# Transform parts in the order sine, cosine, sine, cosine, and a row's write issued one ReLU later

## The chip, the cores and the metric

The kernel runs on one core of a Trainium2 chip. The metric is the device time of the kernel in microseconds (us). One further execution was recorded by the hardware profiler; all durations of single instructions come from it.

The engines are named as in the profile: PE is TensorE (matmuls; PEld are its weight loads), DVE is VectorE, ACT is ScalarE, POOL is GpSimd, SP is SyncE, which only issues DMAs here. A small q behind a name (ACTq) is that engine's sequencer, which works through the engine's instructions in their order; where one waits, all behind it wait.

## The reference

```python
def _attn_ref(x):                      # x: 8 x 3008 x 256
    X = np.fft.fft(x, axis=1)
    X = np.fft.fft(X, axis=2)
    return X.real.astype(np.float32)

def _moe_ref(x, w_in, w_out):          # x: 24064 x 256, w_in: 256 x 2048, w_out: 2048 x 256
    h = np.maximum(x @ w_in, 0.0)
    return (h * h @ w_out).astype(np.float32)
```

A two-dimensional Fourier transform of each of 8 batches, of which the real part is kept, then a feed-forward layer with a squared ReLU on all 24,064 rows.

## The kernel before

**Folding.** The input is real, so the output rows k and 3008 − k are found together. DVE folds each batch by symmetry (`fold_steps`), and the transform along the sequence is done for half of the rows: a cosine part `zc` and a sine part `zs`, both 128 partitions (features, folded too) by columns, one column for a pair of output rows. The transform along the features is merged into the weights of the first layer: `gh` has three blocks of 128 x 2048. For a pair, block 0 times `zc` plus block 1 times `zs` gives the first layer's result of row k (`pq`, L729 and L730). Block 2 times `zs`, added in the same PSUM tile, turns it into that of row 3008 − k (`turn`, L735). Block 2 is −2 times block 1, but for one feature, d=128, which lies in partition 0 of `zs` and keeps its sign.

**Units.** The columns are made in 16 units, two for each batch. In what follows the unit of the odd k is called early, that of the even k late. An early unit has 752 columns and 12 matmuls on `od`, a late one 753 columns and 20 matmuls on `xt`, `yt` and `spn` (both kinds L480). A unit is four parts: cosine or sine, each in a first half and a second half. `z_steps(u)(part, h)` gives the matmuls of one part: part 0 is the cosine, part 1 the sine, h the half. An early unit has three matmuls to each of the four. A late one has four to a cosine part and six to a sine part.

**A part's work.** The first half goes into a PSUM bank (pool `ps_z`, two buffers), and ACT copies it to `es` (L485). The second half is then added into the same bank, so its first matmul must wait for that copy. ACT copies the sum to `zc` or `zs` (L489): these are the unit's first 376 or 377 columns. DVE computes 2·es − sum (L496, `minus`): the other 376. Early units also need a column that a small matmul and a DVE copy make (`nyq`, L375 to L377, into the sine's half of `od`), late ones small POOL copies (`nyq8`, L423 to L425, into what the sine's first half reads).

**Windows and steps.** The columns are worked through in 25 windows, w = 0 to 24, most of them 512 wide (the first six are 240, 512, 376, 376, 512 and 448). A window has eight steps; step s does 256 of the 2048 hidden features for the window's columns. The code issues, engine by engine, in the order in which it is written: this is a schedule by hand (`manual_schedule`), so each engine runs its instructions in the order of the calls. In a usual step this is:

1. `pq(s)`: four matmuls into a PSUM tile (pool `ps_h`, two buffers).
2. `square(s, 0)`: the first ReLU on ACT (L739) into an `h1` tile (three buffers), then its square into `h2`, on DVE (L744) or, for the steps in `by_act`, on ACT (L742).
3. `others(s)`: fold work that is due; an eighth of the second layer of the window before (`ffn2_steps`: L618, 16 matmuls a group of 128 rows, in odd steps ACT's copy `osb`, L633, and the stores, L598, on SP's queue; `osb` has three buffers); and a seventh of the transform jobs of the unit that starts in the next window.
4. `turn(s)`: two matmuls; then `square(s, 1)`: the second ReLU and its square.

In windows 3 and 5 to 24, steps 1 up to 3, 4 or 5 are *halved* (`halved(w)`): ACT reads the PSUM tile only by copies, `sn` (L757, −2 times the sine's product) and `hd` (L766), and DVE forms the second row from the first (L774, L779, L787 to L789). There the d=128 feature must be added back: `row_sum` multiplies row 0 of `zs`, spread over all partitions in `eb`, by a weight (L774, twice a step) and adds it.

**The row.** `row_spread(w)` makes `eb` for window w in two DMAs: ACT's queue writes row 0 of `zs` to DRAM (`zr`, L579), and SP's queue, behind it, reads it back to all 128 partitions (`eb`, L581). It is called in step 6 of the window before. The write waits for the columns of `zs` that it reads, those of ACT and, where the window has some, those of DVE. In windows 0 and 4, two steps go together (`ng` = 2), and `row_spread` has another place.

**The order of the parts.** L721 lists a unit's jobs as cosine first half, sine first half, sine second half, cosine second half. `spread` deals the list in equal shares to steps 0 to 6 (in window 4 to steps 4 to 6, in window 1 all to step 6). Units are made in these windows:

| units | windows |
|---|---|
| early (12 matmuls) | 1, 6, 9, 11, 14, 17, 20 |
| late (20 matmuls) | 3, 4, 7, 10, 13, 16, 19, 22 |

The first early unit is made ahead of window 0, by calls of its own.

Of the kernel before, what the change touches and what calls it, by code (L numbers as in the profile page):

```python
# [19 lines left out]
def rev_dim(ap, i):  # L20

    dims = [list(d) for d in ap.ap]
    step, cnt = dims[i]
    dims[i] = [-step, cnt]
    return bass.AP(tensor=ap.tensor, offset=ap.offset + step * (cnt - 1), ap=dims)
# [3 lines left out]
def kernel(  # L29
# [51 lines left out]
    NW = len(wins)  # L81
# [372 lines left out]
    def zwin(w):  # L454
        if w not in zc:
            zc[w] = zp.tile([P, WN], F16, name="zc", tag="zc")
            zs[w] = zp.tile([P, WN], F16, name="zs", tag="zs")
        return zc[w], zs[w]
# [67 lines left out]
    def run(*jobs):  # L526
        for j in jobs:
            j()
# [45 lines left out]
    def row_spread(w):  # L574

        wn = wins[w][1]
        t = eb[w] = tmp.tile([P, WN], F16, name="eb", tag="kf")
        zr = drp.tile([1, WN], F16, name="zr", tag="zr")
        nc.scalar.dma_start(out=zr[0:1, 0:wn], in_=zwin(w)[1][0:1, 0:wn])  # L579
        src = zr[0:1, 0:wn]  # L580
        nc.sync.dma_start(out=t[:, 0:wn], in_=bass.AP(tensor=src.tensor, offset=src.offset, ap=[[0, P], [1, wn]]))  # L581
# [84 lines left out]
    def plan(w):  # L666

        if w < 3 or w == 4:
            return (), ()
        return PLAN[min(2, 2 * (w in fold_at) + (w in first_at) + (w in late_at))]  # L670

    def halved(w):

        return plan(w)[0]
# [4 lines left out]
    for w in range(NW):  # L679
# [4 lines left out]
        lo, hi = 0, NST - 1  # L684
# [4 lines left out]
        elif w == 1:  # L689
# [3 lines left out]
            lo, hi = 6, 7  # L693
# [24 lines left out]
        zj, zl = [], []  # L718
        for u in need[w + 1]:
            zu = z_steps(u)  # L720
            zj += [(zu, 0, 0), (zu, 1, 0), (zu, 1, 1), (zu, 0, 1)]  # L721
        f2 = ffn2_steps(*old) if old else []
        phs = {}

        def pq(s):
            ph = phs[s] = ps_h.tile([P, 2, 512], F32, name="ph", tag="psh")
            for a in range(2):
                f0 = (2 * s + a) * P
                nc.tensor.matmul(ph[:, a, 0:wn], gh[:, 0, f0 : f0 + P], zcw[:, 0:wn], start=True, stop=False)  # L729
                nc.tensor.matmul(ph[:, a, 0:wn], gh[:, 1, f0 : f0 + P], zsw[:, 0:wn], start=False, stop=True)  # L730

        def turn(s):
            for a in range(2):
                f0 = (2 * s + a) * P
                nc.tensor.matmul(phs[s][:, a, 0:wn], gh[:, 2, f0 : f0 + P], zsw[:, 0:wn], start=False, stop=True, skip_group_check=True)  # L735

        def square(s, sg):
            h1 = h1p.tile([P, 2, 512], F16, name="h1", tag="h1")
            nc.scalar.activation(h1[:, :, 0:wn], phs[s][:, :, 0:wn], AF.Relu)  # L739
            hv = rev_dim(h1[:, :, 0:wn], 2) if sg else h1[:, :, 0:wn]  # L740
            if sg == 0 and s in by_act:
                nc.scalar.activation(h2[:, 2 * s : 2 * s + 2, 0:wn], hv, AF.Square)  # L742
                return []
            return [lambda: nc.vector.tensor_tensor(h2[:, 2 * s : 2 * s + 2, sg * wn : (sg + 1) * wn], hv, hv, op=ALU.mult)]  # L744
# [5 lines left out]
        def half_q(s):  # L750
            ph = phs[s] = ps_h.tile([P, 2, 512], F32, name="ph", tag="psh")
            for a in range(2):
                f0 = (2 * s + a) * P
                nc.tensor.matmul(ph[:, a, 0:wn], gh[:, 1, f0 : f0 + P], zsw[:, 0:wn], start=True, stop=True)  # L754
            i = ROT[0] % 2
            sn = sns[s] = const.tile([P, 2, 2, WN], F16, name=f"sn{i}", tag=f"w16_{i}")
            nc.scalar.activation(sn[:, 0, :, 0:wn], ph[:, :, 0:wn], AF.Copy, bias=0.0, scale=-2.0)  # L757

        def half_p(s):
            ph, sn = phs[s], sns[s]  # L760
            for a in range(2):
                f0 = (2 * s + a) * P
                nc.tensor.matmul(ph[:, a, 0:wn], gh[:, 0, f0 : f0 + P], zcw[:, 0:wn], start=False, stop=True, skip_group_check=True)  # L763
            hd = tmp.tile([P, 2, 2 * WN], F16, name="hd", tag=("tt", "tm")[ROT[0] % 2])
            ROT[0] += 1
            nc.scalar.activation(hd[:, :, 0:wn], ph[:, :, 0:wn], AF.Copy, bias=0.0, scale=1.0)  # L766
            hds[s] = hd

        def row_sum(s):

            sn = sns[s]

            def row(a):
                nc.vector.tensor_scalar(out=sn[:, 1, a, 0:wn], in0=eb[w][:, 0:wn], scalar1=wv[:, 2 * s + a : 2 * s + a + 1], scalar2=None, op0=ALU.mult)  # L774

            return [
                lambda: row(0),
                lambda: row(1),
                lambda: nc.vector.tensor_tensor(sn[:, 0, :, 0:wn], sn[:, 0, :, 0:wn], sn[:, 1, :, 0:wn], op=ALU.add),  # L779
            ]  # L780

        def halves(s):

            sn, hd = sns[s], hds[s]
            hv = hd[:, :, 0 : 2 * wn]
            return [
                lambda: nc.vector.tensor_tensor(rev_dim(hd[:, :, wn : 2 * wn], 2), hd[:, :, 0:wn], sn[:, 0, :, 0:wn], op=ALU.add),  # L787
                lambda: nc.vector.tensor_scalar(out=hv, in0=hv, scalar1=0.0, scalar2=None, op0=ALU.max),  # L788
                lambda: nc.vector.tensor_tensor(h2[:, 2 * s : 2 * s + 2, 0 : 2 * wn], hv, hv, op=ALU.mult),  # L789
            ]  # L790

        def others(s):
            for j in at[s]:
                j()
            for j in spread(f2, s, NST):
                j()
            for j in post[s]:
                j()
            if s == lo:
                zl[:] = [j for zu, part, h in zj for j in zu(part, h)]  # L800
            if s >= lo:
                for j in spread(zl, s - lo, hi - lo) if s < hi else []:
                    j()


        ng = 2 if w == 0 or wins[w - 1][1] < 384 < wn else 1
        for s0 in range(0, NST, ng):
            ss = range(s0, s0 + ng)
            left = halves(s0 - 1) if s0 - 1 in two else []
            if s0 in two:  # L810
                half_q(s0)
                for j in [j for p in zip(left or [run] * 3, row_sum(s0)) for j in p]:
                    j()
                others(s0)
                half_p(s0)
                continue
            for s in ss:
                pq(s)
            for s in ss:
                run(*(left[0:2] + square(s, 0) + left[2:3]))  # L820
            if s0 == hi - 1 and ng == 1 and w + 1 < NW and halved(w + 1):
                row_spread(w + 1)
            others(s0)
            for s in ss:
                turn(s)
            for s in ss:
                run(*square(s, 1))
            for s in ss[1:]:
                others(s)
            if s0 < hi <= s0 + ng - 1 and w + 1 < NW and halved(w + 1):  # L830
                row_spread(w + 1)
# [33 lines left out]
```

## Time and profile before

| | us |
|---|---|
| time, median of 3 runs | 620.66 (619.44 to 620.81) |
| the profiled execution | 619.07 |
| its span, first to last instruction | 617.1 |
| PE busy | 587.7 |
| ACT busy | 517.6 |
| DVE busy | 498.6 |
| POOL busy | 77.3 |
| DMA engines, mean rate | 81 GB/s |

The span is what the profile divides into busy and idle time; 1.97 us of the execution lie outside it. TensorE's granted clock was 0.998 of full speed. The times of matmuls overlap, as each is listed from its start to the end of its results, so a stall is read from the starts of two matmuls in a row. In the list of waits a line says who waited for whom, with the total in us, the number of waits and the longest. In a timeline a line gives the start, the duration, the engine, the line of the kernel and the tiles (what is written, then what is read), and in brackets the engine's idle time before it and what ended it; "x2" are two such instructions in a row.

A window of 512 columns takes about 24.4 us: the late units' transforms in windows 10, 13, 16 and 19 start at 242.27, 315.68, 389.08 and 462.49 us, three windows apart.

### The profile page before, as it was taken

The page shows a single profiled execution, that of the slowest core. Times are in us where ns is not written, and L with a number is a line of the kernel's source. Part 1 is how long each engine was busy: PE and PEld are TensorE (multiplying, and loading weights), DVE is VectorE, ACT ScalarE, POOL GpSimd, SP SyncE. Part 2 cuts the span into 40 slices and gives each one's busy share as a digit, 9 for nine tenths or more (in the row PEclk, how much of TensorE's full clock was granted, in tenths as well). Part 3 has the DMA queues.
Part 4 walks back from the last instruction along what each step waited for, and adds up shares of the span by engine and source line. Part 5 has one row for each costly group of instructions (what it writes and reads, how often), then busy time and mean ns, then how long its engine had stood idle before and what let it go on. Part 6 is the DMA issues. An engine that isn't in the chain of part 4 may idle for free.

```text
span 617.1 us, 11655 instructions
## 1 busy us (share of the span) xinstructions
PE 587.7 (95%) x4400; PEld 424.0 (69%) x4400; DVE 498.6 (81%) x870; ACT 517.6 (84%) x673; POOL 77.3 (13%) x125
## 2 busy tenths in 40 slices
PE   5899999999899999999999999999999999999996
PEld 2456776776677777677776767677776776766785
DVE  7886688696888887969978799768987698797980
ACT  7786788888889889889898898888987988979871
POOL 5352200002001022020011100211000200100000
PEclk9999999999999999999999999999999999999999
DMA  8937121164214522631145311552212411111122
GB/s 145 219 71 144 61 68 35 43 150 104 52 38 83 151 85 57 134 112 59 37 106 121 91 49 46 98 131 81 52 31 66 111 52 44 55 47 42 58 58 65
DMA packets 39593, 50.22 MB, mean 81 GB/s; under 512 B 4572, under 2 KB 33393, under 8 KB 39537
## 3 DMA queue, kind: packets, MB, share of 16 engines
q0 software_dynamic: 9344, 22.14, 17.9%
q1 hardware_dynamic: 29923, 27.11, 15.3%
q8 instruction: 34, 0.56, 0.4%
q10 hardware_dynamic: 270, 0.23, 0.1%
q14 instruction: 22, 0.18, 0.1%
HBM read 36.29 MB, written 27.86 MB: 104 GB/s over the span
## 4 chain that ended last, share of the span: by engine, by line
PE 57%; ACT 15%; DVE 13%; issue 8%; DMA 5%; POOL 1%; SPq 0%; ACTq 0%; DVEq 0%; POOLq 0%
PE po L618 33%; ACT h L739 7%; PE ph L735 4%; PE ph L763 4%; PE ph L729 4%; PE ph L730 4%; PE ph L754 4%; PE pz L480 2%; DVE hd L787 2%; DMA out_dram<-osb 2%; DVE h L744 2%; ACT osb L633 2%; ACT hd L766 2%; DVE hd L788 2%; DVE sn L779 2%
## 5 line engine op out<-in xcount | busy, mean ns | idle before, releaser
L618 PE MATMUL po<-wout,h 128*128 128x256 f16 (+1 forms) x3024 | 361.7, 273 | 0.0
L618 PEld LDWEIGHTS <-h 128*128 128x128 f16 (+1 forms) x3024 | 296.5, 98 | 71.3
L739 ACT ACTIVATE h<-ph 128x1024 f16<-128x1024 f32 (+4 forms) x236 | 217.0, 961 | 27.4 <-PE ph L735 18.3
L744 DVE TENSOR_TENSOR h<-h 128x1024 f16<-128x1024 f16 (+4 forms) x173 | 109.5, 641 | 67.4 <-ACT h L739 65.3
L766 ACT ACTIVATE hd<-ph 128x1024 f16<-128x1024 f32 (+3 forms) x82 | 81.4, 992 | 28.1 <-PE ph L763 27.3
L789 DVE TENSOR_TENSOR h<-hd 128x2048 f16<-128x2048 f16 (+3 forms) x82 | 96.5, 1177 | 0.4
L729 PE MATMUL ph<-zc,gh 128*128 128x512 f16 (+4 forms) x236 | 85.2, 363 | 1.3 <-ACT h L739 0.5
L730 PE MATMUL ph<-zs,gh 128*128 128x512 f16 (+4 forms) x236 | 85.1, 363 | 0.4 <-ACT zs L489 0.4
L757 ACT ACTIVATE sn<-ph 128x1024 f16<-128x1024 f32 (+3 forms) x82 | 81.2, 991 | 0.4 <-DVE hd L787 0.2
L787 DVE TENSOR_TENSOR hd<-hd,sn 128x1024 f16<-128x1024 f16 (+3 forms) x82 | 54.9, 670 | 20.0 <-ACT hd L766 14.3
L735 PE MATMUL ph<-zs,gh 128*128 128x512 f16 (+4 forms) x236 | 65.4, 363 | 4.8 <-ACT h L739 3.2
L633 ACT ACTIVATE osb<-po 128x512 f32<-128x512 f32 (+3 forms) x95 | 54.6, 579 | 18.2 <-PE po L618 13.2
L742 ACT ACTIVATE h<-h 128x1024 f16<-128x1024 f16 (+3 forms) x63 | 64.8, 1029 | 2.0
L774 DVE TENSOR_SCALAR sn<-eb,wv 128x512 f16<-128x512 f16 (+3 forms) x164 | 54.3, 342 | 4.2 <-DMA eb<-zr 2.8
L779 DVE TENSOR_TENSOR sn<-sn 128x1024 f16<-128x1024 f16 (+3 forms) x82 | 54.5, 664 | 2.2
L788 DVE TENSOR_SCALAR hd<-hd 128x2048 f16<-128x2048 f16 (+3 forms) x82 | 54.7, 667 | 0.7
L763 PE MATMUL ph<-zc,gh 128*128 128x512 f16 (+3 forms) x164 | 47.3, 370 | 1.7 <-ACT sn L757 1.0
L754 PE MATMUL ph<-zs,gh 128*128 128x512 f16 (+3 forms) x164 | 47.4, 370 | 0.0
L730 PEld LDWEIGHTS <-gh 128*128 128x128 f16 x236 | 23.0, 97 | 25.5 <-issue 2.4
L729 PEld LDWEIGHTS <-gh 128*128 128x128 f16 x236 | 23.0, 97 | 24.8 <-DVE zc L496 1.1
L423 POOL COPY xt<-xt 128x2 f16<-128x2 f16 x16 | 6.0, 402 | 212.2 <-DVE xt L406 212.2
L735 PEld LDWEIGHTS <-gh 128*128 128x128 f16 x236 | 22.3, 97 | 13.2 <-issue 7.9
(121 smaller groups left out, 374.2 us busy)
## 6 DMA issues: line engine op xcount, KB each, us to landing
out_dram<-osb SPq DMA_DIRECT2D x77, 128.0 KB
xo<-in_x_dram POOLq DMA_DIRECT2D x7, 768.0 KB
scr<-ev POOLq DMA_DIRECT2D x8, 390.0 KB, 3.3
eb<-zr SPq DMA_DIRECT2D x18, 128.0 KB
rb<-scr POOLq DMA_DIRECT2D x16, 130.0 KB
out_dram<-osb SPq DMA_DIRECT2D x12, 94.0 KB
w<-in_moe_w_in_dram POOLq DMA_DIRECT2D x2, 512.0 KB
wout<-in_moe_w_out_dram POOLq DMA_DIRECT2D x1, 1024.0 KB
```

The costliest lines, as they stand in the source:

```text
L618: nc.tensor.matmul(po[0:m, j * D : (j + 1) * D], h2[:, fc, q : q + m], wout16[:, fc, :], start=(fc == 0), stop=(fc == NFC - 1))
L729: nc.tensor.matmul(ph[:, a, 0:wn], gh[:, 0, f0 : f0 + P], zcw[:, 0:wn], start=True, stop=False)
L730: nc.tensor.matmul(ph[:, a, 0:wn], gh[:, 1, f0 : f0 + P], zsw[:, 0:wn], start=False, stop=True)
L735: nc.tensor.matmul(phs[s][:, a, 0:wn], gh[:, 2, f0 : f0 + P], zsw[:, 0:wn], start=False, stop=True, skip_group_check=True)
L739: nc.scalar.activation(h1[:, :, 0:wn], phs[s][:, :, 0:wn], AF.Relu)
L744: return [lambda: nc.vector.tensor_tensor(h2[:, 2 * s : 2 * s + 2, sg * wn : (sg + 1) * wn], hv, hv, op=ALU.mult)]
L754: nc.tensor.matmul(ph[:, a, 0:wn], gh[:, 1, f0 : f0 + P], zsw[:, 0:wn], start=True, stop=True)
L757: nc.scalar.activation(sn[:, 0, :, 0:wn], ph[:, :, 0:wn], AF.Copy, bias=0.0, scale=-2.0)
L763: nc.tensor.matmul(ph[:, a, 0:wn], gh[:, 0, f0 : f0 + P], zcw[:, 0:wn], start=False, stop=True, skip_group_check=True)
L766: nc.scalar.activation(hd[:, :, 0:wn], ph[:, :, 0:wn], AF.Copy, bias=0.0, scale=1.0)
L787: lambda: nc.vector.tensor_tensor(rev_dim(hd[:, :, wn : 2 * wn], 2), hd[:, :, 0:wn], sn[:, 0, :, 0:wn], op=ALU.add),
L789: lambda: nc.vector.tensor_tensor(h2[:, 2 * s : 2 * s + 2, 0 : 2 * wn], hv, hv, op=ALU.mult),
```

## The change

Two edits. In the job list of a unit, the first two entries change places, so that the parts come as sine first half, cosine first half, sine second half, cosine second half. And in step 6 of a window, `row_spread` is called behind `turn` and the second `square`, instead of ahead of `others`.

```diff
@@ -718,7 +718,7 @@
         for u in need[w + 1]:
             zu = z_steps(u)
-            zj += [(zu, 0, 0), (zu, 1, 0), (zu, 1, 1), (zu, 0, 1)]
+            zj += [(zu, 1, 0), (zu, 0, 0), (zu, 1, 1), (zu, 0, 1)]
         f2 = ffn2_steps(*old) if old else []
@@ -818,13 +818,13 @@
                 run(*(left[0:2] + square(s, 0) + left[2:3]))
-            if s0 == hi - 1 and ng == 1 and w + 1 < NW and halved(w + 1):
-                row_spread(w + 1)
             others(s0)
             for s in ss:
                 turn(s)
             for s in ss:
                 run(*square(s, 1))
+            if s0 == hi - 1 and ng == 1 and w + 1 < NW and halved(w + 1):
+                row_spread(w + 1)
             for s in ss[1:]:
                 others(s)
```

Every engine has as many instructions as before. PE runs the same matmuls with the first halves exchanged, and in late units, whose sine parts are longer, other matmuls fall into a step. On ACT the copies `es` change places in the same way, and the write of the row stands one ReLU later in 20 of 21 windows (window 4 has its own place for it). On SP the broadcast moves behind four stores in window 6 and keeps its place elsewhere.

## The prediction

> **What bounds the kernel now.** I read the shares of busy time first, then the list of waits, then the timelines of TensorE (PE), ScalarE (ACT) and VectorE (DVE) in each window that runs a transform.
>
> ```profile
> PE 587.7 (95%) x4400; PEld 424.0 (69%) x4400; DVE 498.6 (81%) x870; ACT 517.6 (84%) x673; POOL 77.3 (13%) x125
> ...
> PE pz L480 <- ACT es L485: 7.6, 9, 1.0
> ACT osb L633 <- DMA zr<-zs: 1.8, 1, 1.8
> DVE sn L774 <- DMA eb<-zr: 2.8, 2, 2.2
> ```
>
> PE has almost no idle time, so only what delays PE counts, and the first wait is nearly pure PE time: nine times a transform's matmul waits for ACT to copy the bank that it adds to (7.6 us). Six of the nine are alike, in step 3 of windows 7, 10, 13, 16, 19 and 22 (178.46 to 545.18 us). PE in window 10:
>
> ```profile
> 250.71 0.25 PE L480 MATMUL pz<-cos,spn 128*128 128x94 f16 x2
> 251.93 0.24 PE L480 MATMUL pz<-sin,xt 128*128 128x188 f16 x1 [0.98 <-ACT es L485]
> ...
> 258.26 0.25 PE L480 MATMUL pz<-cos,spn 128*128 128x94 f16 x2
> 258.35 0.24 PE L480 MATMUL pz<-cos,xt 128*128 128x188 f16 x1
> ```
>
> Where nothing waits, the matmul behind such a pair starts 0.09 us after it (258.26 to 258.35); in step 3 it starts 1.22 us after (250.71 to 251.93). So one stall costs PE 1.13 us. ACT meanwhile runs an output copy and then the copy that is awaited:
>
> ```profile
> 250.91 0.60 ACT L633 ACTIVATE osb<-po 128x512 f32<-128x512 f32 x1 [0.24 <-PE po L618]
> 251.40 0.48 ACT L485 ACTIVATE es<-pz 128x377 f32<-128x377 f32 x1
> 252.64 1.02 ACT L766 ACTIVATE hd<-ph 128x1024 f16<-128x1024 f32 x1 [0.76 <-PE ph L763]
> ```
>
> ACT idles 0.76 us behind it, for PE: neither is the bound there, they wait for each other in turn. The second wait stands once on ACT, in step 6 of window 6:
>
> ```profile
> 162.50 0.21 ACTq L579 DMA_DIRECT2D zr<-zs  x1
> 162.90 0.60 ACT L633 ACTIVATE osb<-po 128x512 f32<-128x512 f32 x1 [1.78 <-DMA zr<-zs]
> ...
> 165.75 0.59 PE L735 MATMUL ph<-zs,gh 128*128 128x512 f16 x2 [1.73 <-ACT h L739]
> ...
> 162.22 0.60 DVE L496 SCALAR_TENSOR_TENSOR zs<-es,pz 128x102 f16<-128x102 f32 x2
> 162.74 0.69 DVE L744 TENSOR_TENSOR h<-h 128x1024 f16<-128x1024 f16 x1
> ```
>
> The row's write needs the sine columns that DVE finishes at 162.4; ACT's queue stands still behind it, both ReLUs come late, and PE waits 1.73 us at the next turn.
>
> **Part 1, the order of the four transform parts.** No instruction is added or removed: per unit the same matmuls, two es copies and two L496s. Before, the sine's second half came straight behind its first, and had to wait for ACT's copy of the same bank. After, four (late units) or three (early units) cosine matmuls stand between, and the sine's copy has all of a step or more to run. A late unit's 20 matmuls are dealt over steps 0 to 6 as 2, 3, 3, 3, 3, 3, 3: the sine's first six end in step 2 instead of step 3, so the wait in step 3 goes; the cosine's copy takes the sine's old place in ACT's queue, and its second half comes two steps later. The sums, by window:
>
> - Windows 7, 10, 13: the 1.13 us goes, and with it 0.12 us in step 2 (PE L763 waits for ACT's sn copy at 248.10: the es copy leaves ACT's step 1 for step 2, which has no output copy). 1.25 us each, 3.75 us. What is late next is DVE, which runs without a gap from 247.2 to 260.4 and does not get faster. ReLU tiles have three buffers: the first ReLU of step 6 (260.7) needs the one that DVE's L744 reads until 259.1, so there is 1.55 us of cover. DVE itself gets 0.36 us (hd of step 1 starts 0.36 us earlier, no copy of 0.48 us ahead of it), so 1.25 us fits.
> - Window 16: the same 1.25 us, but window 17 gives some back. There DVE waited for the row's broadcast already (first L774 at 418.82, 1.34 us idle), on transfers that crowd the queue and do not shift with PE. I take DVE 0.9 us later against PE; its L789 of step 5 ends 437.97 and PE's output matmuls need it at about 438.4, so 0.4 us is covered, 0.5 is paid: 0.7 us kept.
> - Window 19: DVE starts 2.19 us late (below), and its L744 ends at 480.70, just as the ReLU of step 6 starts (480.88). No cover: 0.1 us.
>
> ```profile
> 467.23 0.62 DVE L774 TENSOR_SCALAR sn<-eb,wv 128x512 f16<-128x512 f16 x2 [2.19 <-DMA eb<-zr]
> ...
> 557.97 0.60 DVE L496 SCALAR_TENSOR_TENSOR zc<-es,pz 128x16 f16<-128x16 f32 x2
> ...
> 558.19 0.39 PE L729 MATMUL ph<-zc,gh 128*128 128x512 f16 x1
> ```
>
> - Window 22 has five halved steps, and the next window needs 16 of the columns that DVE makes last: the last two lines above, L496 at 557.97 and the matmul behind it at 558.19 (due at 558.12). Only DVE's own 0.36 us is gained.
> - Window 3: stall of 0.74 us, but its end waits for DVE too (0.34 us at 95.66, DVE without a gap from 81.4): 0.
> - Window 4: 0.74 us at 112.95; DVE idles 1.67 us at 115.27, so it is kept: 0.74.
> - Window 1: all twelve matmuls in one step. Two es copies in a row end at 50.40 and 50.88; the sine's second half may then start at 50.47 instead of 50.93: 0.45.
>
> The sine going first asks for its inputs a step earlier. The Nyquist column (L377) ends 1.4 to 2.5 us before the first transform matmul of early units, GpSimd's copies (L424) 1.1 to 5 us before that of late units. I take 0, and up to 1 us a unit if that cover goes.
>
> **Part 2, the row's write.** 20 of 21 writes move behind one ReLU (window 4 has its own place for it). The issue itself is 0.215 us on ACT's sequencer, beside a running instruction: 0.
>
> In window 6 the hold moves from in front of output copy, cosine copy and second ReLU to in front of the next ReLU. These three then run 161.1 to 163.0 while the wait ends at 162.5. But the next ReLU needs a buffer that DVE's L744 frees at 163.43, so it starts 163.5 instead of 164.66: 1.15 us of the 1.73.
>
> The price is a later row: 0.2 to 1.4 us (to the start of the next L739 in each window). It lands 1.1 us after its issue in quiet stretches (window 8: issued 211.17) and up to 3.65 in busy ones (window 16: 408.54, SP's broadcast behind it at 412.24). The broadcast lands mostly 3.0 to 3.5 us after that (5.4 for window 19, where SP's issue waits behind a store until 461.67, so that a later write costs nothing there). Before DVE's first L774 this leaves 1.5 to 5.3 us in all windows but 5, 17 and 19. So it is hidden but for window 17 (counted above); unhidden, it would be up to 1.4 us of DVE time a window, of which chains of five halved steps cover 0.4 (window 17) to 0.9 (window 14). On SP the broadcast passes four stores in window 6 only, with 3.9 us to spare: 0. In window 2 output buffers wait for stores behind the broadcast (ACT idle 0.90 us at 75.51): −0.2.
>
> [...]
>
> **Sum:** 3.75 + 0.7 + 0.1 + 0.36 + 0 + 0.74 + 0.45 + 1.15 − 0.2 = 7.05 us. The profiled execution took 619.07 us (span 617.1 and 1.97 around it): 612.0. It lies 1.6 us under the median of 620.66, from which the forecast for the median is **613.6 us**.
>
> **Rivals.**
> - *DVE is the bound in all late units* (chance 0.20). For: its chains without a gap, 3.9 us a halved step against PE's 2.9. Against: no L618 waits for DVE, idle time in steps 6 to 0. Each of six windows then gains 0.36, windows 2 and 17 lose 0.7: 2.2 + 0.74 + 0.45 + 1.15 − 0.7 = 3.8, 616.8 us.
> - *All covers hold* (0.12). 6 × 1.25 + 2 × 0.74 + 0.45, and both holds of ACT that reach PE (1.73, and 0.45 before 557.69): 11.6 us, 609.1. For: DVE has idle time in every window. Against: the buffers and columns named above.
> - *The reorder only moves the wait* (0.05): the second half of the cosine waits instead, or the sine waits for its inputs (up to 1 us in each of nine units). Against: two steps of cover. Within 0.2% of before, about 620.
> - *Slower: the late row starves DVE* (0.08). Place: the first L774 of a window. If each broadcast took window 19's 5.4 us instead of 3.2 and the write came 1.4 later, the twelve windows with under 3.6 us to spare would start DVE some 1.75 us late, less 0.6 of cover: 14 us lost against 7 gained, 627.6. It decides from about 0.7 us of uncovered lateness in each of twelve. Against: PE did not stall behind the 2.19 us at 467.
>
> **How the numbers follow.** The forecast (611 to 616) has 0.55. The next two, 609.1 with 0.12 and 616.8 with 0.20, lie in the range, with 0.6 us below and the spread of the three runs (1.4 us) above: 608.5 to 618.2, which leaves out the last two rivals and some edges. 0.2% (1.2 us) is about what a measurement of this kernel can tell from no change. Faster 0.87, same 0.05, slower 0.08.
>
> **What would show it.** Right: PE's waits for es under 1 us in all, no gap in step 3 of windows 7 to 16, ACT's 1.78 us gone and some 0.7 us left before the turn in step 7 of window 6. Wrong: PE L618 or ACT L739 waiting for DVE in windows 8 to 18, or L774 waiting for the broadcast in more than four windows.

## The result and the profile after

The changed kernel took 610.2 us (median of 4 runs, 609.66 to 612.05); the kernel before took 620.05 us beside it (4 runs, 619.21 to 620.81). The ratio is 0.9847, 95% interval 0.982 to 0.9874: faster, by 9.85 us between the medians (1.5%). The profiled execution took 609.66 us (before 619.07), its span is 607.6 us (617.1).

The shares of busy time of the changed kernel, and its list of waits (total us, times, longest us):

```profile
PE 585.7 (96%) x4400; PEld 423.4 (70%) x4400; DVE 497.9 (82%) x870; ACT 518.0 (85%) x673; POOL 79.0 (13%) x125
```

```profile
DVE sn L774 <- DMA eb<-zr: 5.8, 3, 3.0
...
PE ph L763 <- ACT sn L757: 2.1, 6, 0.6
...
ACT sn L757 <- DVE hd L787: 1.9, 3, 0.9
```

PE has the same matmuls. Its idle time, the span less its busy time, fell from 29.4 to 21.9 us; its busy time is 2.0 us less, as a part of each stall is listed as busy (of the 1.13 us between the starts, 0.98 were listed as idle). `PE pz L480 <- ACT es L485`, 7.6 us before, is gone from the list, and so is ACT's wait of 1.8 us for `zr`. The last two lines have grown, from 1.0 and 0.2 us, and DVE's wait for the broadcast from 2.8 to 5.8 us.

**Where the time went, window by window.** A window's length is the distance from its first `pq` matmul on PE to the next window's. It repeats to 0.01 us from one execution to the next almost everywhere, so it tells far smaller differences than the time of the whole kernel. In all windows that are not listed it changed by less than 0.01 us.

| window | change of length, us | forecast of the step |
|---|---|---|
| 1 | −0.47 | −0.45 |
| 2 | 0.00 | +0.2 |
| 3 | −0.03 | 0 |
| 4 | −0.96 | −0.74 |
| 6 | −1.85 | −1.15 |
| 7 | −1.14 | −1.25 |
| 10, 13, 16 | −1.25 each | −1.25 each |
| 17 | **+1.57** | +0.5 |
| 18 | −0.04 | 0 |
| 19 | **−1.25** | −0.1 |
| 22 | −0.30 | −0.36 |
| 23 | −0.51 | 0 |

They sum to 8.7 us. The other 0.8 us of the 9.5 us between the two spans lie behind PE's last matmul: there the span of before goes on for 5.32 us and that of the changed kernel for 4.56, because before's last output copy waited for a store (1.59 us). Of the eleven runs below, ten end in 4.57 to 4.73 us and one, with the changed order, in 5.52, so I take this for chance and no part of the change.

**Step 3 of a late unit.** PE in window 10 of the changed kernel, at the place where it stood still for 0.98 us before:

```profile
252.59 0.25 PE L480 MATMUL pz<-cos,spn 128*128 128x94 f16 x2
252.68 0.24 PE L480 MATMUL pz<-cos,xt 128*128 128x188 f16 x1
252.76 0.59 PE L735 MATMUL ph<-zs,gh 128*128 128x512 f16 x2
```

The starts are 0.09 and 0.08 us apart and there is no bracket: the cosine's matmuls run through.

**Step 6 of window 6.** First ACT, then DVE, then PE:

```profile
160.43 1.02 ACT L739 ACTIVATE h<-ph 128x1024 f16<-128x1024 f32 x1
161.08 0.21 ACTq L579 DMA_DIRECT2D zr<-zs  x1
161.39 1.02 ACT L739 ACTIVATE h<-ph 128x1024 f16<-128x1024 f32 x1
```

```profile
160.79 0.60 DVE L496 SCALAR_TENSOR_TENSOR zs<-es,pz 128x102 f16<-128x102 f32 x2
161.31 0.68 DVE L744 TENSOR_TENSOR h<-h 128x1024 f16<-128x1024 f16 x1
```

```profile
162.47 0.59 PE L735 MATMUL ph<-zs,gh 128*128 128x512 f16 x2
```

The second ReLU (160.43) now runs ahead of the row's write. The first of the two L496 makes the sine columns that the row needs and ends at 161.04, the write goes at 161.08, and the next ReLU follows at 161.39 with nothing waited for. It starts while DVE is still busy with L744 (161.31 to 161.99), and PE's next turn at 162.47 has no idle time ahead of it.

**Window 17.** DVE, ACT and PE of the changed kernel, where the new waits are:

```profile
412.27 0.61 DVE L774 TENSOR_SCALAR sn<-eb,wv 128x512 f16<-128x512 f16 x2 [2.98 <-DMA eb<-zr]
...
417.45 0.69 DVE L787 TENSOR_TENSOR hd<-hd,sn 128x1024 f16<-128x1024 f16 x1
```

```profile
418.24 1.02 ACT L757 ACTIVATE sn<-ph 128x1024 f16<-128x1024 f32 x1 [0.76 <-DVE hd L787]
...
421.90 1.02 ACT L757 ACTIVATE sn<-ph 128x1024 f16<-128x1024 f32 x1 [0.94 <-DVE hd L787]
```

```profile
419.31 0.59 PE L763 MATMUL ph<-zc,gh 128*128 128x512 f16 x2 [0.57 <-ACT sn L757]
...
422.97 0.59 PE L763 MATMUL ph<-zc,gh 128*128 128x512 f16 x2 [0.57 <-ACT sn L757]
```

This is a chain to be read from top to bottom: the broadcast lands late, so DVE starts 2.98 us after it could. There are two `sn` tiles (L755), so ACT may write a step's `sn` only when DVE's L787 has read that of two steps before, and it waits 0.76 and 0.94 us. PE needs ACT to have read its PSUM tile, and stands still twice, 0.73 us each time by the distance of its starts; 0.11 us more go in the step ahead of these.

### The profile page after: what moved, and what is told of

It is laid out like the page before. It is cut to its first block, busy times and chain, and to the rows that moved or that the text cites. A ratio compares the mean times of both kernels' runs of the same rounds, so it can differ in the third digit from the quotient of the medians.

```text
span 607.6 us, 11662 instructions
## 1 busy us (share of the span) xinstructions
PE 585.7 (96%) x4400; PEld 423.4 (70%) x4400; DVE 497.9 (82%) x870; ACT 518.0 (85%) x673; POOL 79.0 (13%) x125
## 4 chain that ended last, share of the span: by engine, by line
PE 57%; DVE 16%; ACT 10%; issue 9%; DMA 6%; POOL 1%; SPq 0%; ACTq 0%; DVEq 0%; POOLq 0%
PE po L618 33%; PE ph L735 5%; PE ph L729 5%; PE ph L730 5%; ACT h L739 5%; PE ph L763 3%; DVE hd L787 3%; DVE sn L779 3%; PE ph L754 3%; DVE hd L788 3%; DVE sn L774 2%; DMA eb<-zr 2%; PE pz L480 2%; ACT sn L757 2%; DMA out_dram<-osb 2%
## 5 line engine op out<-in xcount | busy, mean ns | idle before, releaser
L618 PE MATMUL po<-wout,h 128*128 128x256 f16 (+1 forms) x3024 | 361.7, 273 | 0.0
L618 PEld LDWEIGHTS <-h 128*128 128x128 f16 (+1 forms) x3024 | 296.6, 98 | 71.3
L739 ACT ACTIVATE h<-ph 128x1024 f16<-128x1024 f32 (+4 forms) x236 | 217.3, 961 | 26.3 <-PE ph L735 15.4
L744 DVE TENSOR_TENSOR h<-h 128x1024 f16<-128x1024 f16 (+4 forms) x173 | 109.1, 642 | 61.6 <-ACT h L739 54.8
L789 DVE TENSOR_TENSOR h<-hd 128x2048 f16<-128x2048 f16 (+3 forms) x82 | 96.6, 1178 | 0.4
L787 DVE TENSOR_TENSOR hd<-hd,sn 128x1024 f16<-128x1024 f16 (+3 forms) x82 | 55.0, 671 | 18.4 <-ACT hd L766 10.7
L774 DVE TENSOR_SCALAR sn<-eb,wv 128x512 f16<-128x512 f16 (+3 forms) x164 | 54.6, 343 | 5.8 <-DMA eb<-zr 5.8
```

Of the source, the lines that this page charges most:

```text
L618: nc.tensor.matmul(po[0:m, j * D : (j + 1) * D], h2[:, fc, q : q + m], wout16[:, fc, :], start=(fc == 0), stop=(fc == NFC - 1))
```

## The experiments

The theory for part 1, called D in the expectations: the stall goes because other matmuls stand between the halves of one part. The rival: because the sine comes first. For window 17 there are three: the later write itself starves DVE (L), the read-back stands in a queue behind stores (Q), the two `sn` tiles pass the lateness on (S). All changes of window lengths below are against the kernel before.

### One part at a time

The order alone (the row's write at its old place), and the row's write alone (the old order of parts):

```diff
             if s0 == hi - 1 and ng == 1 and w + 1 < NW and halved(w + 1):
                 row_spread(w + 1)
             others(s0)
```

> Only the parts' order is changed; the row's write stays ahead of the transform jobs of step 6. Theory L (the late write is what starves VectorE in window 17): window 17 gives back at most 0.5 us instead of 1.57, windows 1, 4, 7, 10, 13, 16 and 19 keep their gains (0.47, 0.96, 1.14, 1.25 each), window 6 keeps its hold (0 instead of 1.85 gained); sum about 620.05 - 8.3 = 611.8, or near the changed kernel. Rival Q (the broadcast lands late in window 17 because the queues do not move with TensorE): window 17 gives back about 1.5 us here too, sum about 613.

> Only the row's write is moved. Both theories: window 6 gains 1.85 us, the stalls at the es copies stay (9 waits, 7 to 8 us). Theory L: VectorE's wait for the broadcast in window 17 grows from 1.3 us towards 3 and TensorE pays up to 1.5 us there; total 618.2 to 620. Rival Q: window 17 as before, total about 618.0. In neither is it slower than before.

The order alone: 611.2 us, ratio 0.987 (0.9845 to 0.9894). The row alone: 616.29 us, ratio 0.995 (0.9933 to 0.9967). With the order alone, ACT's wait in window 6 stays:

```profile
ACT osb L633 <- DMA zr<-zs: 1.8, 1, 1.8
```

The windows show what belongs to which part. Window 6 (−1.86) and window 23 (−0.52) belong to the row: with the order alone both are 0.00. Everything else is the order's, but for window 17: +0.59 with the order alone, 0.00 with the row alone, +1.57 with both. So the two parts add up in all windows but this one. There the order alone lies between what L (at most 0.5) and Q (about 1.5) had me expect, and the row alone, where DVE waits 1.29 us (before 1.34), speaks against L.

### Is it the sine first, or something between the halves?

```diff
-            zj += [(zu, 1, 0), (zu, 0, 0), (zu, 1, 1), (zu, 0, 1)]
+            zj += [(zu, 1, 0), (zu, 0, 0), (zu, 0, 1), (zu, 1, 1)]   # e3: sine outside, cosine halves adjacent
+            zj += [(zu, 0, 0), (zu, 1, 0), (zu, 0, 1), (zu, 1, 1)]   # e5: alternating, cosine first
```

> Order sine first half, cosine first half, cosine second half, sine second half, row's write as in the changed kernel. Theory D (what counts is that other matmuls stand between a part's two halves): the cosine's second half now stands right behind its first, so the stalls are back, for the cosine: 1.13 us each in windows 7, 10, 13, 16, 19, 0.74 in window 4, 0.3 to 0.5 in window 1; about 616 to 617. Rival (sine first, or the row's place, is what gains): no stalls, about 610. The sine is done a step later, so in window 6 the hold of ScalarE may come back (up to 1.9 us).

> Order cosine, sine, cosine, sine, row's write as in the changed kernel. Theory D (other matmuls between a part's halves): no wait for es in late units, the same gains in windows 4, 7, 10, 13, 16 (0.96, 1.14, 1.25 each) as with the sine first. Rival (the sine has to come first): the stalls stay. The sine's second half ends in step 6 instead of 5, so where the row waits for VectorE's sine columns (windows 6 and 22) ScalarE is held in front of the next ReLU, up to 1.4 and 2.2 us as with the adjacent order. Total 610.5 to 613.

Adjacent halves with the sine first: 619.31 us, ratio 0.9983 (0.9968 to 0.9998), nearly all of both gains is lost, where I had expected 616 to 617 us. The list of waits of that run:

```profile
PE pz L480 <- ACT es L485: 7.6, 9, 1.0
...
ACT h L739 <- DVE zs L496: 2.4, 1, 2.4
```

The nine waits are back, with the cosine as their object. Windows 10, 13 and 16 keep 0.46 of the 1.25 us: the 1.13 us in step 3 have returned, but steps 1 and 2 are 0.12 us shorter and the last two steps 0.40. Alternating with the cosine first: 613.93 us, 0.9911 (0.9887 to 0.9934), somewhat above the 610.5 to 613 us that I expected; windows 10, 13, 16 and 19 are shorter by 1.48 to 1.49 us, more than with the sine first. So D holds and the rival falls: for PE it only counts that something stands between.

What the sine's early end is good for shows in the second line. If the sine's second half is the last job, DVE makes the row's columns only in step 6, and the write waits for them. ACT and PE of the adjacent order, in window 22:

```profile
557.45 0.21 ACTq L579 DMA_DIRECT2D zr<-zs  x1
557.71 1.02 ACT L739 ACTIVATE h<-ph 128x1024 f16<-128x1024 f32 x1 [2.38 <-DVE zs L496]
```

```profile
558.78 0.59 PE L735 MATMUL ph<-zs,gh 128*128 128x512 f16 x2 [2.08 <-ACT h L739]
```

The write stands in ACT's queue until DVE is done, the ReLU behind it waits 2.38 us, and PE 2.08 us. With the cosine first that wait is 3.6 us, window 22 is longer by 1.74 us, and window 6 gains 0.45 us instead of 1.85.

### The write earlier: is window 17 starved by the late row?

The write is issued as soon as the sine columns it needs are there (in most windows in step 0 or 5 instead of 6), also in halved steps:

```diff
+        row_at = hi - 1 if by_dve or w < 5 else hi - 2 if need[w + 1] else 0
...
+                if s0 == row_at and w + 1 < NW and halved(w + 1):
+                    row_spread(w + 1)
...
-            if s0 == hi - 1 and ng == 1 and w + 1 < NW and halved(w + 1):
+            if s0 == row_at and ng == 1 and w + 1 < NW and halved(w + 1):
```

> Changed kernel, but the row is written as soon as its columns stand: in step 0 where the window makes no unit, in step 5 where it makes one whose first columns ScalarE writes alone, and as in the changed kernel in windows 6, 9 and 22, where VectorE writes some. Theory L: no wait of VectorE for the broadcast in windows 17 and 19, window 17 gives nothing back, 1.5 us below the changed kernel, about 608.6. Rival Q: the broadcast still lands late in window 17 behind stores and loads, within 0.5 us of the changed kernel.

608.82 us, ratio 0.983 (0.9805 to 0.9856). All windows are as in the changed kernel but for window 17, which gives back 0.66 us instead of 1.57. The row was in DRAM at 402.29 us, yet SP issued the read-back only at 404.69:

```profile
398.15 6.42 SPq L598 DMA_DIRECT2D out_dram<-osb  x5
404.69 1.59 SPq L581 DMA_DIRECT2D eb<-zr  x1
```

```profile
411.44 0.62 DVE L774 TENSOR_SCALAR sn<-eb,wv 128x512 f16<-128x512 f16 x2 [2.07 <-DMA eb<-zr]
```

Five stores hold SP's queue for 6.4 us, and the broadcast takes 6.7 us more. L explains a part at most; the rest points to the queue.

### The read-back past the stores

In window 17 alone, POOL's queue issues the broadcast instead of SP's: with the early write (e8), and with the write where the change put it (e10).

```diff
-        nc.sync.dma_start(out=t[:, 0:wn], in_=bass.AP(tensor=src.tensor, offset=src.offset, ap=[[0, P], [1, wn]]))
+        (nc.gpsimd if w == 17 else nc.sync).dma_start(out=t[:, 0:wn], in_=bass.AP(tensor=src.tensor, offset=src.offset, ap=[[0, P], [1, wn]]))
```

> The kernel with the row written early, and the broadcast of window 17 alone issued from GpSimd's queue instead of SP's. Theory Q (what is left in window 17 is the broadcast's place behind stores in SP's queue, issued 6 us after its write and landing 6.7 us later): it lands by 408, VectorE does not wait, window 17 gives back nothing instead of 0.66 us; about 608.1. Rival (the 16 DMA engines are full in this stretch, whatever the queue): it lands as late as before.

> The changed kernel, the row's write still behind the second ReLU, with nothing but window 17's broadcast read issued on GpSimd's queue instead of SyncE's. Theory Q (the queue behind the few-row stores sets when the broadcast lands): row landed at about 405.4 us as in the changed kernel, broadcast some 4.7 us later at 410.1 us, VectorE's first L774 idle about 0.8 us instead of 2.98, window 17 gives back 0 to 0.2 us instead of 1.57; time about 1.5 us below the changed kernel's, 608.7 us. Theory L (the late write itself starves VectorE): a row later by about 1 us still costs about 0.9 us, window 17 gives back 0.7 to 0.9 us, time about 609.5 us.

Beside them the changed kernel ran once more:

> The changed kernel once more, beside the two others on the same chip: every window's length as in its first profile within 0.05 us (window 17 longer by 1.57 us, window 6 shorter by 1.85 us, windows 10, 13, 16 and 19 shorter by 1.25 us), median 610 to 611 us. If its window 17 gives back another amount, transfers' landing is chance and not the queue.

Early write and POOL's queue: 608.03 us, 0.9824 (0.9797 to 0.9851); DVE does not wait and window 17 gives back 0.00. Late write and POOL's queue: 610.1 us, 0.9835 (0.9814 to 0.9856). DVE in window 17 of the latter:

```profile
412.98 0.35 DVE L774 TENSOR_SCALAR sn<-eb,wv 128x512 f16<-128x512 f16 x1 [0.73 <-DMA eb<-zr]
```

It waits 0.73 us, and the window still gives back 0.00. So the late write alone does no harm: L, as I had stated it (0.7 to 0.9 us given back), falls, and Q holds. Only together with SP's queue does it add something, between 0.2 and 0.9 us (0.86 and 1.57 in the changed kernel against 0.66 with the early write). The 608.7 us that I expected of this run did not come out as its median: its four executions had mean clocks of 0.994 to 0.999 (last section), and the one with 0.999 took 608.58.

The repeat was not as I expected: 610.39 us, 0.9846 (0.9826 to 0.9867), all windows within 0.02 us of the first profile but window 17, which gave back 0.86 us instead of 1.57. Transfers land differently from one execution to the next. That weakens a reading of single differences of some 0.5 us there, the 0.66 of the early write among them, and asks for the rule behind them. It is simple: where DVE's first L774 starts, counted from the window's first matmul, against what the window gives back:

| kernel | L774 starts after, us | given back, us |
|---|---|---|
| early write, POOL | 5.06 | 0.00 |
| late write, POOL | 5.87 | 0.00 |
| row alone | 6.44 | 0.00 |
| before | 6.49 | 0.00 |
| adjacent halves | 6.73 | 0.17 |
| order alone | 7.15 | 0.59 |
| early write, SP | 7.22 | 0.66 |
| changed, repeated | 7.41 | 0.86 |
| cosine first | 7.90 | 1.34 |
| changed | 8.12 | 1.57 |

In these ten profiles, from 6.55 us on each microsecond costs a microsecond. The kernel before was 0.06 us short of that point.

From its issue to its landing, window 17's broadcast took 5.7 to 6.8 us on SP behind stores in seven kernels of the table, 4.7 us there with adjacent halves, and 4.6 to 4.7 us on POOL's queue (two). The row's own write, on ACT's queue, took 3.65 to 4.37 us in all ten, whether it was issued 5.7 or 2.5 us ahead of the window.

What is late is one part of the read. The trace records the landing of a DMA in up to sixteen parts. In the kernel before, 19 of the 21 broadcasts have all sixteen on record: in 18 of them the last part comes at most 0.4 us behind the fifteenth, in window 19's 2.15 us. Window 17's broadcast is recorded in full in the other twelve profiles. There the fifteenth part landed 3.2 to 4.2 us after the issue, on SP's queue as on POOL's, and the last one 1.5 to 3.4 us behind it on SP's queue (nine) but 0.7 to 1.3 us on POOL's (three). Stores ahead of it land in few parts: in the changed kernel one of 59 rows landed in a single part, at 409.24 us, one of 94 rows in two, at 407.44 and 411.30, and the last part of the broadcast at 412.25. What the last part waited for the trace does not tell.

### A third sn tile

```diff
-            i = ROT[0] % 2
-            sn = sns[s] = const.tile([P, 2, 2, WN], F16, name=f"sn{i}", tag=f"w16_{i}")
+            i = ROT[0] % 3
+            sn = sns[s] = const.tile([P, 2, 2, WN], F16, name=f"sn{i}", tag=("w16_0", "w16_1", "sn_c")[i])
```

(To make room, tiles used only at the start share its memory.)

> Changed kernel with a third sn tile (three small set-up tiles share memory for it). Theory S (in window 17 TensorE stands because ScalarE's sn copy waits for VectorE to release one of two sn tiles): the two waits of 0.74 us at L763 in window 17 go. VectorE's own chain is as late as before, so the output matmuls of window 18's first step (L618) wait for its L789 instead, about 1.2 us: the total stays within 0.5 us of the changed kernel. Rival (the two waits come from the late hd copies or from TensorE itself): the 0.74 us stay where they are.

610.37 us, 0.984 (0.982 to 0.986). DVE waits 2.46 us for the broadcast (2.98 and 2.27 in the two profiles of the changed kernel), but window 17 gives back 0.00 and window 18 gives back 0.54 us, where PE waits for something else:

```profile
PE po L618 <- DVE h L789: 0.8, 2, 0.6
```

So the two tiles are what passes DVE's lateness to PE (S holds). With three it reaches PE through `h2`, later and smaller. This second path is the one that the prediction had named.

### Fewer halved steps where DVE ends last, and all together

A smaller plan of halved steps in windows 3, 17 and 22 (e7, on the early write), and in 3 and 22 alone with window 17's read on POOL's queue (e9):

```diff
+        if w in (3, 22):
+            return PLAN[1]
```

> The kernel with the row written early, and in windows 3, 17 and 22 four halved steps instead of five. Each such step takes about 3.9 us (3.0 in window 3) off VectorE's chain, less one square, and adds 0.43 us (0.31) to TensorE. Theory (VectorE is the bound at the ends of windows 3, 17 and 22): the waits at the first matmul of the next window (1.25 and 1.37 us) and in window 17 (0.66) go, 3.3 less 1.2: about 2.0 us below the kernel with the early row, 606.8. Rival (ScalarE, which gets ReLUs for copies, takes VectorE's place): no gain, 608.8 or more.

> The kernel with the early row and window 17's broadcast on GpSimd's queue, and besides it five halved steps fewer or later in windows 3 and 22 alone (the plan that the run with fewer halved steps gave to windows 3, 17 and 22). Theory D+L+Q: the gains are separate windows' gains, so they add: window 17 gives nothing back (0.00 against before), windows 3 and 4 together 0.43 us shorter than after, window 22 0.88 us shorter than after: profiled span about 606.0 - 1.3 = 604.7 us, median about 606.7 us, ratio to before about 0.980. Rival (VectorE carries its lateness from one window to the next): window 17 or 23 pays part of it back, span 605.5 us or more.

The first: 608.5 us, 0.9825 (0.9802 to 0.9849), against the 606.8 that I expected. Windows 3 and 4 together are 0.42 us shorter than with the early write alone and window 22 0.87 us, but window 17 gives back 1.03 instead of 0.66, of which window 18 regains 0.32. By windows it gains 1.25 us instead of 2.0; the medians, of executions at different clocks, show 0.3 of it. The second keeps what gained: **607.16 us** (5 runs), ratio 0.981 (0.9789 to 0.9831), profiled span 604.9 us. By windows: 3 and 4 together −1.43, 17 0.00, 22 −1.18, 23 −0.53, PE's last matmul 11.46 us earlier than before, against 8.71 in the changed kernel. The gains of single windows add up and nothing is carried on.

## Why the prediction was right, and where its sum was not

The direction and the mechanism held: 613.6 us was forecast with 608.5 to 618.2, and 610.2 measured. The sum of the windows came out at 8.7 us instead of 7.05, and single terms were off by up to 1.15 us, with opposite signs: that the sum is as near as it is owes something to luck. Of the 3.4 us between forecast and median, 1.7 lie in the windows, some 0.7 behind PE's last matmul and outside the span, and 1.0 in the step from the profile to the median.

- **Windows 7, 10, 13, 16: right** (1.25 each; measured 1.14 and three times 1.25). The stall of 1.13 us and the 0.12 us in step 2 both went; the order alone shows the same numbers, and adjacent halves bring the stall back.
- **Window 19: wrong, 0.1 instead of 1.25.** The step that failed is the cover. I held that the ReLU of step 6 cannot start before DVE's L744 ends, since it needs the `h1` tile which that frees. In the changed kernel, ACT, then DVE:

```profile
472.06 1.95 ACT L739 ACTIVATE h<-ph 128x1024 f16<-128x1024 f32 x2
```

```profile
473.39 0.68 DVE L744 TENSOR_TENSOR h<-h 128x1024 f16<-128x1024 f16 x1
```

  The second of the two is the ReLU in question; it started at about 473.0, before the L744 that I had it wait for began (473.39). The code has three `h1` tiles, and I let the ReLUs take them in turn; by these starts this ReLU took another one than the L744 was to read. Which one the profile does not tell. DVE started 2.21 us late in this window, as before, and PE lost nothing by it.
- **Window 6: mis-sized, 1.15 instead of 1.85**, by the same mistake: I let the next ReLU wait for DVE's L744 until 163.43. It did not wait for it, and all of the 1.73 us came back, with 0.12 more.
- **Window 17: mis-sized, 0.5 instead of 1.57** (0.86 in the repeat). I took DVE 0.9 us later and 0.4 us of cover through L789 and L618. The cover was 0.06 us, because the `sn` tiles come first; and DVE came 0.9 to 1.6 us later against PE (8.12 and 7.41 us after the window's start instead of 6.49). In the first profile 0.95 us of this are the row's later issue, counted from the window's start, 0.44 its longer way, and the rest the broadcast's. The trace of before showed the two tiles (L755) and the distance; I looked at one path only.
- **Windows 8 and 17, the later row.** The prediction held it hidden everywhere but in window 17. Window 8, whose row took 3.27 us from its issue to its landing, paid 0.00; window 17 paid 1.07 us (0.36 in the repeat) more than my term. Window 17's row took 3.65 to 4.37 us, whenever it was issued; what decided was SP's queue, where the broadcast took 5.7 to 6.8 us behind stores, against 4.6 to 4.7 on POOL's.
- **Window 22, window 3: right.** 0.30 for 0.36, 0.03 for 0. There DVE ends last, as the smaller plan confirms: with fewer halved steps window 22 shrinks by 0.88 us more, and 3 and 4 together by 0.44. PE's and its weight loads' waits for DVE's last columns are these of the changed kernel's list; PE waits 1.08 us at the end of window 3 and 1.21 us at the end of window 22:

```profile
PEld L729 <- DVE zc L496: 3.2, 2, 1.7
...
PE ph L729 <- DVE zc L496: 2.3, 2, 1.2
```

- **Window 4: 0.96 instead of 0.74.** Step 5, with the stall, is 0.73 us shorter, step 0 0.31 us, where PE no longer waits for a ReLU, and step 1 0.09 us longer; why the first two steps changed I have not shown. Windows 3 and 4 trade with each other: the cosine first gives −1.20 and +0.01.
- **Window 23: not foreseen, 0.51.** It comes of the second hold of ACT, 0.45 us of PE's time at the end of window 22 by my own reading, that I had counted for the rival "All covers hold" and left out of my sum. With the row moved, that hold goes, but PE waits for DVE's columns instead, so window 22 itself gains nothing by it (0.00 in the row alone). What is gained lies in the first two steps of window 23, where PE's waits for ACT of 0.11 and 0.14 us are gone. It is the row's: the order alone leaves it.
- **Window 2: 0.2 lost forecast, 0.00 measured.** Window 1: right.
- **From the profile to the median:** I added 1.6 us, as the three runs of before stood above their profile. Later medians of before are 619.3 to 620.05, less than 1 us above it.

Of the signs named, no L618 and no L739 waits for DVE in windows 8 to 18, and L774 waits for the broadcast in three windows (5, 17 and 19); the 0.7 us that were to be left in window 6 are gone too.

Of the rivals, "DVE is the bound in all late units" fell (five of six windows shrank by 1.14 us or more, though window 17 gave back what 16 had gained), "the reorder only moves the wait" fell (one wait of 0.10 us for `es` is left, in window 1), "slower" fell, as the broadcast came late for PE in one window only. "All covers hold", 609.1, was nearer than my own forecast: all held but those of windows 3, 17 and 22.

## What to carry to other kernels

Where an accumulation must wait for another engine's copy of the same bank, put any other work between the halves: here a stall of 1.13 us went with either part first, and was back with adjacent halves. Which part goes first mattered only for who needs its result (window 22 was 1.74 us longer with the cosine first). Before a cover is counted, list every tile that the late engine must free, with its number of buffers, and compare start times with the trace: a wait for a tile that was never there cost 1.85 us of this sum, and tiles not looked at 1.07. When compute moves ahead, look at the read that lands closest to its need: it may stand in a queue behind stores, and a queue without stores was worth more here (window 17 gave back 0.00) than an earlier write (0.66).

## What the runs showed of the hardware

**The clock at the start.** Window 0 began at 21.4 to 21.8 us in seven of the thirteen profiles and at 22.6 to 24.7 us in six. The stretches (length, then busy us of PE, PEld, DVE, ACT, POOL; then the granted clock, the DMA share, GB/s) of the changed kernel's first profile and of its repeat, each followed by PE's first matmul on the weights:

```profile
12.00:16.00 4.00, 2.02 (x12) 0.85 (x11) 3.39 (x5) 2.50 (x3) 0.00 (x0) 1.00 1.04 168
16.00:20.00 4.00, 3.57 (x20) 1.76 (x19) 3.64 (x6) 2.80 (x5) 1.65 (x2) 1.00 1.33 199
```

```profile
15.55 0.60 PE L438 MATMUL pg<-w,c_all 128*128 128x512 f16 x2 [1.20 <-DMA w<-in_moe_w_in_dram]
```

```profile
12.00:16.00 4.00, 1.46 (x8) 0.71 (x8) 3.58 (x5) 1.73 (x3) 0.00 (x0) 0.88 1.04 161
16.00:20.00 4.00, 4.00 (x11) 1.52 (x10) 3.09 (x3) 1.42 (x2) 1.85 (x2) 0.50 1.34 200
```

```profile
15.83 1.04 PE L438 MATMUL pg<-w,c_all 128*128 128x512 f16 x2 [2.25 <-DMA w<-in_moe_w_in_dram]
```

In the seven, PE waited at most 1.50 us for its weights, and the clock was 1.00 in all stretches from 12 to 24 us. In the six it waited 1.59 to 2.59 us; the clock was 0.85 to 0.99 in the mean from 12 to 16 us and 0.50 to 0.71 from 16 to 20, the pair of matmuls above took 1.03 to 1.04 us instead of 0.60 to 0.61, and all that follows came up to 3 us later. The spread of the runs goes with the clock: with a mean clock of at least 0.998 the changed kernel took 609.01 to 609.75 us, with 0.993 to 0.995 it took 610.12 to 612.05. What lowered the clock was not shown; I made no experiment on it.

**Some stores landed in one part, 4.8 to 12.5 us after their issue.** In the traces of both kernels a store of 128 rows landed in sixteen parts, one of 94 rows in two, those of 59, 79 and 113 rows in one. In the kernel before, two stores of 79 and 113 rows, issued at 454.55 and 456.65 us, landed at 461.88 and 466.81, 4.93 us apart, which would be some 23 rows of 1 KB in a microsecond for the second. The next store, of 15 rows, held SP's queue from 456.99 to 461.67 us, and window 19's broadcast, issued at 461.78, let DVE start at 467.23 us. Such stores are what stands ahead of the broadcasts of windows 17 and 19; that it is they that held the queue no run isolates.

**An issue was not held by the ReLU ahead of it.** ACT of the changed kernel, in step 6 of window 16:

```profile
401.31 0.22 ACTq L579 DMA_DIRECT2D zr<-zs  x1
...
401.73 1.94 ACT L739 ACTIVATE h<-ph 128x1024 f16<-128x1024 f32 x2
```

The first of these two ReLUs stands ahead of the write in the code, and starts 0.42 us after it: the issue did not wait for the ReLU to run. So the write moved by less than the ReLU's length (0.95 us, counted from window 17's start, against 1.02).
